# Ranks and allowances in a planned instruction order: softmax maximum and exponential first, later dates for what follows them

## Chip, cores, metric

One core of one Trainium2 chip. The time is device microseconds of one execution; lower is better. The kernel before took 956.38 us (median of three runs, 956.17 to 956.78).

## What is computed

Block-causal attention, then two MLPs, in fp32:

```python
scores = scale * q @ k.T            # 4 batches, 8 heads, 576 rows, head size 64
scores = where(block_i >= block_j, scores, -1e9)      # blocks of 64
attn = exp(scores - max) / (sum + 1e-9)
x = (attn @ v) as (2304, 512)
x = leaky(x @ w_in) @ w_out         # 512 -> 2048 -> 512, leak 0.01
out = silu(x @ w2_in) @ w2_out
```

## The kernel before

**Stages.** The 2304 tokens are cut into six blocks of 384 (0 to 5). The first MLP of a block is 16 steps: a first layer (L1427 to L1429), its gate on ACT (L1475), a high and a low part of the gated value (g_hi on ACT or DVE, g_lo on DVE, L384), and a second layer (L1447). Every fp32 product of block 1 and later is three matmuls of high and low parts. While the layers of block b run, the attention of block b+1 is worked in between them; a block's first layer needs that block's whole x. Block 0 and the attention of block 1 use a simpler form (`start`, `pair_unit`); blocks 2 to 5 use `unit`. After the attention (some 520 us into the span) come the rest of the first MLP and the second MLP (L1681 to L1683, L1844), which the change does not touch.

**One unit of attention** (`unit`, L1053) is up to 128 query rows of one head, or the last 64 rows of two heads. Its chain, with the names used below:
- **scores**, PE, L1084, into one of two PSUM banks `s`; 576 keys are done as two pieces of 288
- **max**, DVE: memset of the masked corner (L1092), then the reduction (L1094; L1096 and L1098 for two pieces)
- **exp**, ACT, L1102, out of the bank, which is then free for the scores after next
- **norm**, DVE, L1109 to L1112
- **p_hi**, ACT or DVE, L1116 or L1118, then **p_lo**, DVE, L1121
- a transposing DMA by the queue of SP, L1130
- **weighing** (`weigh_all`, L1198), PE, L1145 to L1147, all units of a group into the one bank `x`
- **x_top**, ACT or DVE, L858 or L860, then **x_sum**, DVE, L864: the two halves of that bank, evacuated and added; the next group's weighing waits for them
- x in a high and a low part (L373 or L375, then L384 `l<-x,h`), which the first layer reads

A head's keys and queries are loaded by SP (L792, L830) and split in parts by ACT and DVE (k_lo is L384 `k<-kqr,k`, q_lo L807).

**The order** is made on the host by `Schedule` (L69). Every piece of work is a task with engines and modelled durations, the tasks it needs, and a rank. The planner steps through modelled time. When a task ends, its users may be ready after a hop (`HOP`) plus the task's `lag`; a task joins its engine's queue when it has been ready for `slack` ns; a free engine takes the lowest rank that waits:

```python
heapq.heappush(waiting, (t.ready + t.slack + (self.HOLD if n else 0), order[id(t)], n, e, t))
...
u.ready = max(u.ready, t.end + (self.HOP[e] + t.lag if u in t.users else 0))
```

What comes out is a fixed order of instructions on each engine; the waits in the program are those of the data. So ranks, lags and slacks change no wait and no duration, they only change places in the order. Gates and their parts have rank GATE (-1000) plus their step, scores, weighings, transposes and x_top/x_sum SHORT (-500) plus a rank, the rest of the attention its plain rank (60 and more). Before the change scores and weighings have a slack of 700, max and exp the plain rank, and lags exist only on loads and transposes.

Of the kernel before, what the change touches and what calls it, by code (L numbers as in the profile page):

```python
# [38 lines left out]
SLACK = 700  # L39
# [10 lines left out]
ORDER = (1, 2, 6, 7, 5, 4, 3)  # L50
BEHIND, LAG = 6, 2500
KQ_LAG, V_LAG, PT_LAG = 2500, 2500, 1500
KQR, KR, QR, VR = 960, 1728, 2048, 1792
PR, HLR, PTR = 1408, 2304, 2304

# [140 lines left out]
def freed(*regions):  # L196

    return [t for r in regions for o in r.before for t in o.users]
# [35 lines left out]
def attn_mlp_mlp(  # L234
# [103 lines left out]
    plan = Schedule()  # L338


    def act(n, psum=False, pointers=0):
        return 0.833 * n + (52 if psum else 94) + 93 * pointers

    def dve(n, pointers=0):
        return Both(1.042 * n + 68 + 61 * pointers)

    def dve_psum(n):
        return 1.042 * n + 68

    def dve2x(n, pointers=0):  # L350
        return Both(0.521 * n + 68 + 61 * pointers)

    def mm(n):
        return max(107, n / 2.4) + 13.5
# [22 lines left out]
    def copy_on(n, psum=False):  # L377
        return {"ACT": act(n, psum), "DVE": dve_psum(n) if psum else dve2x(n)}
# [346 lines left out]
    def attention(blk):  # L725
# [6 lines left out]
        def rank_at(k):  # L732
            first = blk == 1
            return (blk - 1 + k / n_ticks * (ATT1 if first else ATT_SLOPE)) * NF + (ATT0 if first else ATT)
# [113 lines left out]
        def take(hd, both, group, at, t0, t1, done_by):  # L848

            d0 = D * (hd.h % 2)  # L850
            cols, to = slice(at, at + t1 - t0), slice(t0 - hd.q0, t1 - hd.q0)

            def x_top(e):
                if both.x is None:
                    both.x = rp.tile([P, NB], F32, tag="x32", name="x32")
                o, i = both.x[d0 : d0 + D, to], group.x[D:, cols]
                if e == "ACT":
                    nc.scalar.activation(o, i, AF.Copy, scale=1.0 / PS)  # L858
                else:
                    nc.vector.tensor_scalar(o, i, 1.0 / PS, None, op0=ALU.mult)  # L860

            def x_sum(e):
                o = both.x[d0 : d0 + D, to]
                nc.vector.scalar_tensor_tensor(  # L864
                    o, group.x[:D, cols], 1.0 / PS, o, op0=ALU.mult, op1=ALU.add
                )

            rk = SHORT + rank_at(done)
            t_top = plan.add(copy_on(t1 - t0, True), [*done_by, *(pairs[-1] if pairs else ())], rk, x_top)
            t_sum = plan.add({"DVE": dve_psum(t1 - t0)}, [t_top], rk, x_sum)  # L870
            group.evac.append(t_sum)
            both.evac.append(t_sum)
# [18 lines left out]
        def two_heads(hds, both):  # L891

            nonlocal done
            assert hds[0].q0 == 0 and hds[0].q1 % P == 0
            chunks = hds[0].q1 // P
            for cs in (range(chunks - 1), range(chunks - 1, chunks)):
                before = groups[-1] if groups else None
                groups.append(Group())
                group, width = groups[-1], len(cs) * P
                for n, c in enumerate(cs):  # L900
                    pair_unit(hds, c * P, (n * P, width + n * P), rank_at(done), group)
                    done += 2 * P
                done_by = weigh_all(group, before)
                for j in (0, 1):
                    take(hds[j], both, group, j * width, cs[0] * P, cs[-1] * P + P, done_by)
            take_pair(hds[0], both)

        for i in range(0, len(todo), 2):
# [21 lines left out]
            for bank in banks:  # L930
                before = groups[-1] if groups else None
                groups.append(Group())
                group, at, cols = groups[-1], 0, []
# [119 lines left out]
    def unit(parts, per, rk, group, group_before):  # L1053

        u = Unit()
# [4 lines left out]
        w = n // n_pieces  # L1060
# [5 lines left out]
        r_st = st_ring.take(8)  # L1066
# [11 lines left out]
        def scores(e, piece):  # L1078
            k0, k1 = cut[piece]
            s = u.s[piece] = next_s()  # L1080
            for i, (hd, c0, _) in enumerate(parts):
                c = c0 - hd.q0
                for j, a in enumerate((c, hd.np + c)):
                    nc.tensor.matmul(  # L1084
                        s[:, :w], hd.q[:, a : a + P], hd.k[:, k0:k1],
                        start=i + j == 0, stop=i == len(parts) - 1 and j == 1,
                    )

        def row_max(e, piece):
            last = piece == n_pieces - 1  # L1090
            if per > BLK and last:
                nc.vector.memset(u.s[-1][:BLK, w - BLK : w], MASKED)  # L1092
            if n_pieces == 1:
                nc.vector.tensor_reduce(nm[:rows], u.s[0][:rows, :n], axis=AX.X, op=ALU.max, negate=True)  # L1094
            else:
                nc.vector.reduce_max(m2[:rows, piece : piece + 1], u.s[piece][:rows, :w], axis=AX.X)  # L1096
                if last:
                    nc.vector.tensor_reduce(nm[:rows], m2[:rows], axis=AX.X, op=ALU.max, negate=True)  # L1098

        def expo(e, piece):  # L1100
            k0, k1 = cut[piece]
            nc.scalar.activation(  # L1102
                p[:rows, k0:k1], u.s[piece][:rows, :w], AF.Exp, bias=nm[:rows], accum_out=s2[:rows, piece : piece + 1]
            )
# [46 lines left out]
        t_max, s_last = [], before.t_s if before else None  # L1151
        for i in range(n_pieces):
            def first(e, i=i):
                scores(e, i)

            def second(e, i=i):
                row_max(e, i)

            deps = [*split, *s_users[-2]] if len(s_users) > 1 else [*split]
            time = 2 * m * mm(w)  # L1160
            u.t_s = s_last = plan.add({"PE": time}, deps, SHORT + rk, first, [s_last] if s_last else ())
            s_last.slack = SLACK
            s_users.append([])
            masked = 165 if per > BLK and i == n_pieces - 1 else 50
            time = masked + dve_psum(w) + (150 if n_pieces > 1 and i else 0)
            t_max.append(plan.add({"DVE": time}, [u.t_s, *t_max, *(() if i else freed(r_st))], rk, second))
        u.t_max = t_max[-1]
        deps = [u.t_max, *freed(r_p)]
        for i in range(n_pieces):
            def third(e, i=i):  # L1170
                expo(e, i)

            u.t_exp = plan.add({"ACT": act(w, True, 2)}, deps, rk, third, [u.t_exp] if i else ())
            s_users[i - n_pieces].append(u.t_exp)
            deps = []
        u.t_norm = plan.add({"DVE": 290 + 90 * (n_pieces - 1)}, [u.t_exp], rk, norm)
        u.t_hi = plan.add(
            {"ACT": act(n, False, 1), "DVE": dve2x(n, 1)}, [u.t_norm, *freed(r_hl)], rk, p_hi, first_units
        )
        u.t_lo = plan.add({"DVE": dve(n, 1)}, [u.t_hi], rk, p_lo)  # L1180
        padded_keys = [u.t_lo]
        if n % P:
# [15 lines left out]
    def weigh_all(group, before):  # L1198

        us = group.units  # L1200
        deps = [t for u in us for t in (u.t_turn, *[t for hd in u.heads for t in hd.v_ready])]
        deps += before.evac if before else [x0_free]

        def values(e):
            for u in us:
                u.values(e)

        t = plan.add({"PE": sum(u.pv_time for u in us) + TRANSIT}, deps, SHORT + us[-1].rk, values)
        t.slack = 0 if group.units[0].native else SLACK
        for u in us:  # L1210
            u.t_pv = t
            u.r_pt.users.append(t)
            for hd in u.heads:
                hd.rv.users.append(t)
        return [t]
# [819 lines left out]
```

## Time and profile before

| | us |
|---|---|
| median of three runs | 956.38 |
| the profiled execution | 956.43 |
| its span, first to last instruction | 954.7 |
| PE busy | 932.2 |
| DVE busy | 808.5 |
| ACT busy | 557.8 |

The profile's busy share of PE counts modelled matmul durations, which overlap; a stop shorter than that overlap isn't seen in it. PEld is the loading of weights, which runs ahead of PE. A line of the timeline or of a group ends, in brackets or behind a bar, with the idle time of the engine just before it and what ended it. In the table of waits the columns are: engine and instruction that waited, what released it, total us, number of times, longest us.

### The profile page before, as it was taken

What the parts mean: (1) busy time and instruction counts of PE and PEld (TensorE: products, weight loads), DVE (VectorE), ACT (ScalarE), POOL (GpSimd) and SP (SyncE); (2) the same over time, 40 slices, a digit from 0 to 9 for tenths busy, and PEclk for the clock granted to TensorE, in tenths of its full rate; (3) what the DMA queues carried; (4) which work ended last, traced back from release to release, by engine and by line L of the source; (5) the groups of instructions that cost most, each with busy time, mean ns of one, the idle gap of its engine ahead of it and who ended that gap; (6) DMA issues with size and microseconds to landing.
All of it is one profiled execution on the core that took longest, in us unless ns stands there. A gap on an engine that the chain in (4) does not pass through costs nothing.

```text
span 954.7 us, 18424 instructions
## 1 busy us (share of the span) xinstructions
PE 932.2 (98%) x6565; PEld 857.5 (90%) x6565; DVE 808.5 (85%) x1885; ACT 557.8 (58%) x1256; POOL 36.0 (4%) x127
## 2 busy tenths in 40 slices
PE   9999999999999999999999999999999999999997
PEld 4556669898899998999999999999999999999997
DVE  6999899988777788888775897989899999888965
ACT  6987758666665676767465765656455642222222
POOL 1000000100000000000000000000000000000000
PEclk9999999999999999999999999999999999999999
DMA  7777728576545575675444633579846544443412
GB/s 228 221 191 209 206 66 186 108 143 122 151 106 110 126 159 140 121 139 152 97 110 112 206 122 125 198 244 311 287 172 232 185 139 138 129 154 111 144 56 89
DMA packets 193771, 149.05 MB, mean 156 GB/s; under 512 B 134160, under 2 KB 171792, under 8 KB 193680
## 3 DMA queue, kind: packets, MB, share of 16 engines
q1 hardware_dynamic: 193680, 147.89, 56.4%
q8 instruction: 51, 0.84, 0.4%
q14 instruction: 40, 0.33, 0.1%
HBM read 90.70 MB, written 32.51 MB: 129 GB/s over the span
## 4 chain that ended last, share of the span: by engine, by line
PE 47%; DVE 8%; ACT 3%; issue 2%; DMA 0%; DVEq 0%; ACTq 0%
PE acc L1844 7%; PE s L1844 5%; PE acc L1447 4%; PE acc L1681 3%; PE acc L1682 3%; PE acc L1683 3%; PE x L1844 2%; PE u L1844 2%; PE s L1681 2%; PE s L1682 2%; PE h L1427 2%; PE s L1683 2%; PE h L1429 2%; PE h L1428 2%; PE u L1447 1%
## 5 line engine op out<-in xcount | busy, mean ns | idle before, releaser
L1102 ACT ACTIVATE p<-s,st 128x288 f32<-128x288 f32 (+4 forms) x120 | 62.2, 520 | 53.5 <-DVE st L1094 28.7
L1116 ACT ACTIVATE hl<-p,st 128x576 f16<-128x576 f32 (+5 forms) x91 | 55.9, 617 | 38.5 <-DVE st L1112 19.5
L1121 DVE SCALAR_TENSOR_TENSOR hl<-p,st,hl 128x576 f16<-128x576 f32 (+4 forms) x96 | 60.1, 627 | 18.6 <-ACT hl L1116 14.5
L1084 PE MATMUL s<-k,q 128*128 128x288 f32 (+5 forms) x288 | 66.7, 326 | 9.1 <-ACT p L1102 5.4
L1447 PE MATMUL acc<-ghi,w 128*128 128x384 f32 x255 | 67.1, 339 | 0.0
L1084 PEld LDWEIGHTS s<-k,q 128*128 128x128 f32 x288 | 46.4, 189 | 19.4 <-ACT p L1102 14.0
L1475 ACT ACTIVATE g<-h 128x384 f32<-128x384 f32 x96 | 46.5, 484 | 26.2 <-PE h L1429 24.2
L1427 PE MATMUL h<-h,w 128*128 128x384 f32 x180 | 60.9, 338 | 0.0
L1733 ACT ACTIVATE e<-e 128x384 f32<-128x384 f32 (+1 forms) x72 | 42.7, 626 | 26.2 <-DVE e L1706 20.8
L384 DVE TENSOR_TENSOR glo<-g,ghi 128x384 fp32r<-128x384 f32 x80 | 44.2, 553 | 12.3 <-ACT ghi L373 11.8
L1145 PE MATMUL x<-raw,v 128*128 128x128 f16 (+1 forms) x384 | 54.4, 209 | 0.2
L420 ACT ACTIVATE cy<-raw 128x512 f32<-128x512 f32 x64 | 43.1, 674 | 18.5 <-DVE w L442 6.5
L1429 PE MATMUL h<-h,w 128*128 128x384 f32 x160 | 53.7, 335 | 0.0
L1146 PE MATMUL x<-raw,v 128*128 128x128 f16 (+1 forms) x384 | 53.6, 208 | 0.0
L1428 PE MATMUL h<-l,w 128*128 128x384 f32 x160 | 53.6, 335 | 0.0
L1147 PE MATMUL x<-raw,v 128*128 128x128 f16 (+1 forms) x384 | 53.2, 209 | 0.0
L864 DVE SCALAR_TENSOR_TENSOR x<-x,x 64x128 f32<-64x128 f32 (+3 forms) x96 | 30.3, 315 | 19.6 <-ACT x L858 18.2
L1447 PEld LDWEIGHTS acc<-ghi,w 128*128 128x128 f32 x255 | 44.8, 188 | 0.3
L384 DVE TENSOR_TENSOR v<-v 128x320 f32<-128x320 f32 (+5 forms) x112 | 44.2, 424 | 0.3
L1145 PEld LDWEIGHTS <-v 128*128 128x128 bf16 x384 | 36.7, 98 | 5.4 <-issue 4.9
L1447 PE MATMUL acc<-glo,w 128*128 128x384 f32 x120 | 40.3, 336 | 0.0
L373 ACT ACTIVATE ghi<-g 128x384 fp32r<-128x384 f32 x76 | 39.6, 521 | 1.1
(385 smaller groups left out, 3080.9 us busy)
## 6 DMA issues: line engine op xcount, KB each, us to landing
raw<-w SPq DMA_DIRECT2D x64, 512.0 KB, 4.6
raw<-g SPq DMA_DIRECT2D x64, 256.0 KB, 3.1
g<-e SPq DMA_DIRECT2D x48, 192.0 KB, 3.1
g<-e SPq DMA_DIRECT2D x24, 384.0 KB, 3.4
kqr<-kq_l SPq DMA_DIRECT2D x16, 480.0 KB, 3.5
kqr<-kq_l SPq DMA_DIRECT2D x16, 416.0 KB, 3.3
v<-vL SPq DMA_DIRECT2D x32, 160.0 KB, 3.2
y<-yT SPq DMA_DIRECT2D x12, 384.0 KB, 3.7
```

The lines of the kernel that those rows point to most:

```text
L384: engine[e].tensor_tensor(lo, x, hi, op=ALU.subtract)
L1084: nc.tensor.matmul(s[:, :w], hd.q[:, a : a + P], hd.k[:, k0:k1], start=i + j == 0, stop=i == len(parts) - 1 and j == 1,)
L1102: nc.scalar.activation(p[:rows, k0:k1], u.s[piece][:rows, :w], AF.Exp, bias=nm[:rows], accum_out=s2[:rows, piece : piece + 1])
L1116: nc.scalar.activation(hl[:rows, 0, :n], p[:rows], AF.Copy, scale=rc[:rows])
L1121: nc.vector.scalar_tensor_tensor(hl[:rows, 1, :n], p[:rows], rc[:rows], hl[:rows, 0, :n], op0=ALU.mult, op1=ALU.subtract)
L1145: nc.tensor.matmul(g.x[:, o], a, hi, start=j == 0, stop=False)
L1146: nc.tensor.matmul(g.x[:, o], hd.vb[:, j], hi, start=False, stop=False)
L1427: nc.tensor.matmul(h, w1_lo[s.f][:, sl], hi[:, c, : s.n], start=c == 0, stop=False)
L1428: nc.tensor.matmul(h, w1_hi[s.f][:, sl], lo[:, c, : s.n], start=False, stop=False)
L1429: nc.tensor.matmul(h, w1_hi[s.f][:, sl], hi[:, c, : s.n], start=False, stop=c == NC - 1)
L1447: nc.tensor.matmul(s.acc[c][:, : s.n], a, b, start=s.f == 0 and i == 0, stop=s.f == NF - 1 and i == 2)
L1844: nc.tensor.matmul(o, a[:, x], b, start=i == 0 and j == 0 and q == 0, stop=i == NP - 1 and q == 2, skip_group_check=True,)
```

## The change

Six constants and what uses them. Max and exp of a `unit` get the rank CHAIN + rk, that is 100 lower, so that a free engine takes them ahead of other attention work. The slack of scores goes from 700 to 300. Four kinds of task get a lag, by which the planner takes what follows them to be ready later: weighing 800, x_top 400 (not in block 1), norm 300, p_hi 300. (The lag of `t_hi` is on p_hi; its user is p_lo.)

```diff
+CHAIN = -100.0
+S_SLACK = 300
+PV_LAG, TOP_LAG, NORM_LAG, HI_LAG = 800, 400, 300, 300
...
             t_top = plan.add(copy_on(t1 - t0, True), [*done_by, *(pairs[-1] if pairs else ())], rk, x_top)
+            t_top.lag = 0 if blk == 1 else TOP_LAG
...
-            s_last.slack = SLACK
+            s_last.slack = S_SLACK
...
-            t_max.append(plan.add({"DVE": time}, [u.t_s, *t_max, *(() if i else freed(r_st))], rk, second))
+            t_max.append(plan.add({"DVE": time}, [u.t_s, *t_max, *(() if i else freed(r_st))], CHAIN + rk, second))
...
-            u.t_exp = plan.add({"ACT": act(w, True, 2)}, deps, rk, third, [u.t_exp] if i else ())
+            u.t_exp = plan.add({"ACT": act(w, True, 2)}, deps, CHAIN + rk, third, [u.t_exp] if i else ())
...
+        u.t_norm.lag, u.t_hi.lag = NORM_LAG, HI_LAG
...
-        t.slack = 0 if group.units[0].native else SLACK
+        t.slack, t.lag = (0, 0) if group.units[0].native else (SLACK, PV_LAG)
```

## Rows read from the trace of the kernel before

**Rows 1.** The page, part 1: busy time, share, instructions.

```profile
span 954.7 us, 18424 instructions
...
PE 932.2 (98%) x6565; PEld 857.5 (90%) x6565; DVE 808.5 (85%) x1885; ACT 557.8 (58%) x1256; POOL 36.0 (4%) x127
```

**Rows 2.** Windows: stretch, length, busy us by engine, granted clock, DMA share, GB/s.

```profile
120.00:520.00 400.00, 389.34 (x3040) 365.35 (x3039) 330.21 (x954) 262.21 (x685) 30.04 (x110) 1.00 0.57 125
```

**Rows 3.** Waits of PE's matmuls, 120 to 520 us.

```profile
PE s L1084 <- ACT p L1102: 5.4, 10, 1.4
PE s L1084 <- DVE k L384: 3.1, 5, 1.1
...
PE h L1428 <- DVE l L384: 0.5, 1, 0.5
```

**Rows 4.** Line 1084, scores: idle before them (us, times), PEld and PE together.

```profile
ACT p L1102: 19.4, 33
DVE k L384: 3.6, 7
ACT h L373: 2.8, 2
```

**Rows 5.** Timeline of PE around one stop: start us, length us.

```profile
169.47 0.33 PE L1447 MATMUL u<-ghi,e 128*128 128x384 f32 x1
169.64 0.34 PE L1447 MATMUL u<-glo,e 128*128 128x384 f32 x1
171.37 0.53 PE L1084 MATMUL s<-k,q 128*128 128x288 f32 x2 [1.39 <-ACT p L1102]
171.74 0.34 PE L1427 MATMUL h<-h,w 128*128 128x384 f32 x1
```

**Rows 6.** Waits of ACT, 120 to 520 us.

```profile
ACT p L1102 <- DVE st L1094: 28.7, 34, 3.2
ACT p L1102 <- DVE st L1098: 24.3, 22, 3.2
ACT hl L1116 <- DVE st L1112: 19.5, 24, 2.1
ACT x L858 <- PE x L1147: 13.4, 8, 3.6
```

**Rows 7.** Waits of DVE, 120 to 520 us.

```profile
DVE x L864 <- ACT x L858: 16.9, 21, 3.1
DVE hl L1121 <- ACT hl L1116: 14.5, 25, 1.0
...
DVE s L1092 <- PE s L1084: 2.0, 1, 2.0
```

**Rows 8.** Timeline of DVE, 212 to 214 us.

```profile
212.35 0.82 DVE L1121 SCALAR_TENSOR_TENSOR hl<-p,st,hl 128x576 f16<-128x576 f32 x1 [0.72 <-ACT hl L1116]
213.08 0.55 DVE L384 TENSOR_TENSOR glo<-g,ghi 128x384 fp32r<-128x384 f32 x1
...
213.78 0.49 DVE L1094 TENSOR_REDUCE st<-s 128x1 f32<-128x320 f32 x1
```

**Rows 9.** Timelines of PE and ACT beside it.

```profile
211.30 0.54 PE L1084 MATMUL s<-k,q 128*128 128x320 f32 x2
...
214.98 0.54 PE L1084 MATMUL s<-k,q 128*128 128x288 f32 x2 [0.62 <-ACT p L1102]
...
214.31 0.53 ACT L1102 ACTIVATE p<-s,st 128x320 f32<-128x320 f32 x1 [1.48 <-DVE st L1094]
```

**Rows 10.** The page, part 5: the exponentials of the units.

```profile
L1102 ACT ACTIVATE p<-s,st 128x288 f32<-128x288 f32 (+4 forms) x120 | 62.2, 520 | 53.5 <-DVE st L1094 28.7
```

**Rows 11.** Waits of SP's queue, 120 to 520 us: transposes.

```profile
SPq L1130 <- DVE hl L1121: 88.4, 54, 4.1
```

**Rows 12.** Lines 1084 and 1145: durations (ns), first and last start us.

```profile
L1084 PE MATMUL s<-k,q x288: 221/296/657, 127.1 to 505.3; 128*128 128x288 f32 x64, 128*128 128x320 f32 x16, 128*128 128x448 f32 x16, 128*128 128x512 f32 x16
L1145 PE MATMUL x<-raw,v x384: 192/219/233, 155.5 to 515.9; 128*128 128x128 f16 x104, 128*128 128x64 f16 x88
```

**Rows 13.** Timeline of DVE and PE where block 3's first layer begins.

```profile
331.44 0.36 DVE L384 TENSOR_TENSOR l<-x,h 128x192 fp32r<-128x192 f32 x1
...
331.85 0.44 PE L1428 MATMUL h<-l,y 128*128 128x384 f32 x1 [0.46 <-DVE l L384]
```

## The prediction

> **What bounds the kernel now.** I read the page's busy shares first, then the busy time by stretches, then the waits of each engine inside the stretch that the change can reach, and last a timeline of single stops. PE is busy for 932.2 of 954.7 us [rows 1], so it sets the time, and only PE's stops can be won. The change touches blocks 2 to 5 of the attention alone, which run from about 120 to 520 us; there PE is busy for 389.34 of 400 us at a granted clock of 1.00, the 2.4 GHz level [rows 2]. Idle is 400 - 389.34 = 10.7 us. The reader should see how small this is: a perfect order in this stretch gains one or two per cent, no more.
>
> What are the stops? Of PE's matmul waits the largest is scores waiting for an exp, the next scores waiting for k_lo [rows 3]. Both rows together hold 8.5 of the 10.7 us. PE with its weight loads taken together shows more of them: before scores, 19.4 us in 33 stops for an exp, 3.6 us in 7 for k_lo, 2.8 us in 2 for an x part: 25.8 us in 42 stops [rows 4]. The two totals differ because matmul durations overlap. In one stop [rows 5] the layer's matmuls start 0.17 us apart (169.47, 169.64) and are each shown as 0.33 to 0.34 us long, so each stop hides about 0.17 us, and here 1.39 us of idle cost 171.37 - 169.64 - 0.17 = 1.56 us. With 42 stops I put the loss at 10.7 + 42 x 0.17 = 17.8 us, between 10.7 and 25.8. The exp's share by its part in the loads' idle is 19.4 / 25.8 = 0.75: **13.4 us**, with the ends 0.75 x 10.7 = 8.0 and 19.4. After the stop, the layer's matmuls that stood behind the scores start at once (171.74): they were ready.
>
> Here the Trainium skill ("Perfetto Trace Analysis", section Identifying the Most-Contended Engine) says that matmul busy time is a poor measure of distance to the bound and the busy share of weight loads a better one. By that rule the room in this stretch would be 400 - 365.35 = 34.6 us [rows 2] and the exp's share 26 us, my estimate from that page's rule. I keep 13.4, because the loads' idle also holds time in which matmuls were still queued.
>
> **Why the exps are late.** ACT stood idle before them, waiting for the max, for 28.7 us in 34 cases and 24.3 us in 22 [rows 6]: 56 of 120 exps [rows 10]. So DVE had the max late, though it is not full: 330.2 busy of 400 [rows 2]. DVE itself stands still inside its fixed order: 16.9 us for x_top in 21 cases and 14.5 us for p_hi in 25 [rows 7]. One case shows how these join [rows 8, 9]. Scores of 320 columns are done at 211.84 (211.30 + 0.54). DVE waits 0.72 us for p_hi, does p_lo, then g_lo, and starts the max only at 213.78, 1.94 us after the scores. The exp follows 0.04 us after the max, and PE, which wanted the bank, stands 0.62 us until 214.98.
>
> **The change, part by part.**
> - **Max and exp 100 lower in rank.** No instruction is added. In the case above the max passes p_lo and its wait: 213.08 - (212.35 - 0.72) = 1.45 us earlier; it does not pass g_lo, whose rank is lower still. p_lo then comes later by a memset and a reduction, some 0.65 us (213.63, where g_lo ends, to 214.27). Its transpose waits behind it on SP, which already stands 88.4 us for p_lo in 54 cases [rows 11], and loads of keys and values are queued behind the transposes. I cost this at nothing: the weighings begin 28 us after the scores and end 10.6 us after them [rows 12], so there is more than 10 us of work between. If that lead is used up, each of 96 transposes would pass up to 0.65 us on to a weighing, 62 us; nothing near it fits 10 us of lead.
> - **Four lags.** They take a follower off the place where it stops its engine. Mean waits today [rows 6, 7]: x_sum 16.9 / 21 = 0.80 against a lag of 0.4; p_lo 14.5 / 25 = 0.58 against 0.3; p_hi 19.5 / 24 = 0.81 against 0.3; x_top 13.4 / 8 = 1.68 against 0.8. Each covers 0.37 to 0.52 of its mean wait. So about half of 64.3 us of standing in ACT's and DVE's orders goes, between none (other work put there waits too) and all. None of it is PE time by itself; it comes through earlier exps.
> - **Slack 700 to 300.** Scores are placed up to 0.4 us earlier, so a bank must be free 0.4 us earlier too. On a stop that stays this adds up to 0.4 us.
> - The lags make the planned chain 0.8 + 0.4 + 0.3 + 0.3 = 1.8 us longer per unit. Inside a block the lead of 10 us covers it; at a block's end see the second rival.
>
> **The sum.** Where the max was queued behind other DVE work, it comes 1.45 us earlier and the scores 0.4 us: net 1.05 us, against a mean stop of 19.4 / 33 = 0.59 us. Such a stop goes. ACT's rows say that 56 of 120 exps, 47%, were of this kind; I take half of the stops. On the other half, 0.4 us less slack stands against lags of 0.3 to 0.8 us, and I count neither. So half of 13.4 us goes: 6.7 us, between nothing (or the loss of the third rival) and 13.4. From the profiled execution, 956.43 us (1.7 more than its span, and 0.05 from the median), that is **949.7 us**.
>
> **Rivals.**
> 1. *All of it.* Max, exp and lags clear every stop for an exp: 956.4 - 13.4 = 943.0. For: 53 us of ACT's idle before exps has one cause. Against: g_lo and the gates still pass the max, and two banks are as few as before.
> 2. *Given back at the block ends.* A block's first layer needs the last pair's x. It stood 0.46 us for a low part that ended at 331.80 [rows 13], so there the attention has no lead. If the longer chain shows in full, four blocks cost 4 x 1.8 = 7.2 us, and the gain of 6.7 turns into +0.5: 956.9, no change. Against: this is the only such stop in the list [rows 3], 0.5 us, and lags delay only what another task overtakes.
> 3. *Scores too early, slower.* PE's order puts the scores in front of layer matmuls that are ready [rows 5]. If the max comes no earlier in effect, because what it passes was not what held it, each of the 33 stops gets 0.4 us longer: 13.2 us by the loads' count, and by 17.8 / 25.8 about 9.1 us on PE: 965.5. It decides once max plus exp gain less than 0.4 us on average. For: the max itself can then stop DVE waiting for scores; against: that happened once so far, 2.0 us [rows 7], and the one case read closely gains 1.45. The Trainium skill ("PSUM — Partial Sum Buffer", section Engine vs sequencer instructions) states that matmuls start in program order. By that rule the layer's matmuls cannot step past waiting scores, which is this rival's mechanism. The trace agrees: 1.39 us of idle with L1427 right behind.
>
> **Chances.** About 0.2% (1.9 us) is what a measurement can tell from no change. Forecast, between 945 and 954.4: 0.54. First rival, below 945: 0.12. Second, 954.5 to 958.3: 0.16. Third, above 958.3: 0.18. So faster 0.66, same 0.16, slower 0.18. The range, 942 to 959, holds the forecast, more than half of the first rival, the second, and the near end of the third, some 0.8 of the chance.
>
> **What would show it.** Right: idle before scores for an exp falls from 19.4 us in 33 stops to about half; ACT's 53 us before exps falls by at least as much; DVE's waits for x_top and p_hi, 31 us together, fall by half; PE's busy time from 120 to the attention's end comes closer to the stretch, which ends some 6 us sooner; what follows keeps its length. Wrong: exps earlier but PE's stops moved to x parts at block ends (second rival), or more stops before scores with mean above 0.6 us (third).

## The result, and the profile after

The changed kernel takes 947.16 us (median of five runs, 946.88 to 949.66) against 956.38 us before; the ratio is 0.9909, with a 95% interval of 0.9894 to 0.9923. The gain is 9.2 us, where 6.7 was forecast.

The page of the changed kernel, part 1, answers to [rows 1]:

```profile
span 945.8 us, 18395 instructions
...
PE 927.6 (98%) x6565; PEld 857.6 (91%) x6565; DVE 808.8 (86%) x1897; ACT 552.6 (58%) x1244; POOL 37.1 (4%) x127
```

The work is the same but for 12 instructions that passed from ACT to DVE: DVE is busy for 808.8 us as before, PE's weight loads for 857.6. The span is 8.9 us shorter. The same stretch as in [rows 2], by the view of windows:

```profile
120.00:520.00 400.00, 394.39 (x3093) 374.82 (x3093) 336.50 (x978) 262.56 (x684) 31.21 (x110) 1.00 0.58 131
```

PE's idle in it falls from 10.7 to 5.6 us, that of its weight loads from 34.6 to 25.2, and 53 more matmuls fit into the 400 us. Where the gain ends is best read from the first matmul of the second MLP (line 1681 before, 1686 after; columns: durations in ns, first and last start in us). Before:

```profile
L1681 PE MATMUL x<-x,w x48: 333/334/335, 585.8 to 758.2; 128*128 128x384 f32 x48
```

After:

```profile
L1686 PE MATMUL x<-x,w x48: 334/334/343, 576.7 to 749.1; 128*128 128x384 f32 x48
```

The start comes 9.1 us sooner, and from there to the end both need the same time (954.7 - 585.8 = 368.9 and 945.8 - 576.7 = 369.1). So the whole gain lies ahead of the second MLP, as forecast.

What stood before the scores, PE and its weight loads together, answers to [rows 4]:

```profile
ACT p L1106: 13.1, 22
DVE k L387: 1.7, 3
ACT g L1480: 0.7, 1
```

The 25.8 us in 42 stops are 15.5 us in 26. The stops for an exp lost a third (19.4 to 13.1), those for k_lo half, and the two for an x part are gone. The only waits of PE's matmuls themselves, against [rows 3]:

```profile
PE s L1088 <- ACT p L1106: 4.6, 7, 1.2
PE s L1088 <- DVE k L387: 0.9, 2, 0.5
```

In this stretch no layer matmul waits any more, at a block's end or elsewhere. DVE's waits, against [rows 7]; x_top is L861 on ACT and L863 on DVE, x_sum L867:

```profile
DVE glo L387 <- ACT ghi L376: 15.3, 12, 3.6
DVE hl L1125 <- ACT hl L1120: 7.2, 11, 1.1
DVE x L863 <- ACT x L861: 5.6, 6, 2.1
DVE x L867 <- ACT x L861: 5.5, 5, 2.7
```

x_sum's wait falls from 16.9 to 5.5 us (with the x_tops on DVE it is 11.1), p_lo's from 14.5 to 7.2; in exchange g_lo waits longer for its high part, which before was:

```profile
DVE glo L384 <- ACT ghi L373: 6.2, 8, 1.9
```

ACT before the exps, against [rows 6] and the 53.5 us of [rows 10]:

```profile
ACT p L1106 <- DVE st L1098: 28.2, 41, 1.8
...
ACT p L1106 <- DVE hl L1125: 14.5, 11, 2.1
...
ACT p L1106 <- DVE st L1102: 9.1, 8, 2.5
ACT hl L1120 <- DVE st L1116: 8.9, 12, 3.4
ACT x L861 <- PE x L1151: 8.2, 8, 2.2
```

ACT's idle before exps has not fallen: 28.2 + 14.5 + 9.1 = 51.8 us here, 53.0 before. Of it 37.3 us in 49 cases are waits for the max, so these did fall. The 14.5 us in 11 cases are new: there an exp stands until an earlier unit's p_lo (L1125) has read the buffer `p` that it writes to. That ACT's idle falls was to be the sign that the rank works. So three questions were open: which of the three parts carries the gain, whether they need each other, and how much is the luck of another order.

### The profile page after: what moved, and what is told of

Its sections match the earlier page's. It is cut to its first block, busy times and chain, and to the rows that moved or that the text cites. A ratio compares the mean times of both kernels' runs of the same rounds, so it can differ in the third digit from the quotient of the medians.

```text
span 945.8 us, 18395 instructions
## 1 busy us (share of the span) xinstructions
PE 927.6 (98%) x6565; PEld 857.6 (91%) x6565; DVE 808.8 (86%) x1897; ACT 552.6 (58%) x1244; POOL 37.1 (4%) x127
## 4 chain that ended last, share of the span: by engine, by line
PE 49%; DVE 2%; issue 0%; ACT 0%; DVEq 0%
PE acc L1849 8%; PE s L1849 5%; PE acc L1452 5%; PE acc L1686 3%; PE acc L1688 3%; PE acc L1687 3%; PE x L1849 2%; PE u L1849 2%; PE h L1432 2%; PE h L1434 2%; PE h L1433 2%; PE s L1686 2%; PE s L1688 2%; PE s L1687 2%; PE u L1452 2%; PE x L1688 1%
## 5 line engine op out<-in xcount | busy, mean ns | idle before, releaser
L1106 ACT ACTIVATE p<-s,st 128x288 f32<-128x288 f32 (+4 forms) x120 | 62.5, 522 | 53.9 <-DVE st L1098 28.2
L1120 ACT ACTIVATE hl<-p,st 128x576 f16<-128x576 f32 (+5 forms) x87 | 52.8, 616 | 24.6 <-DVE st L1116 8.9
L1125 DVE SCALAR_TENSOR_TENSOR hl<-p,st,hl 128x576 f16<-128x576 f32 (+4 forms) x96 | 59.1, 623 | 7.9 <-ACT hl L1120 7.2
L387 DVE TENSOR_TENSOR glo<-g,ghi 128x384 fp32r<-128x384 f32 x80 | 44.2, 552 | 18.3 <-ACT ghi L376 17.5
L387 DVE TENSOR_TENSOR v<-v 128x320 f32<-128x320 f32 (+4 forms) x112 | 44.9, 423 | 0.7
L1098 DVE TENSOR_REDUCE st<-s 128x1 f32<-128x320 f32 (+3 forms) x72 | 36.3, 504 | 2.3
```

What stands on the lines that cost most here:

```text
L387: engine[e].tensor_tensor(lo, x, hi, op=ALU.subtract)
L1106: nc.scalar.activation(p[:rows, k0:k1], u.s[piece][:rows, :w], AF.Exp, bias=nm[:rows], accum_out=s2[:rows, piece : piece + 1])
L1125: nc.vector.scalar_tensor_tensor(hl[:rows, 1, :n], p[:rows], rc[:rows], hl[:rows, 0, :n], op0=ALU.mult, op1=ALU.subtract)
```

## Experiments

All kernels are the changed one with other constants, so that its lines hold. Times are medians; "against before" is the difference to the kernel before in the same set of runs (medians 956.37 to 956.97).

**Rank alone.**

```diff
-S_SLACK = 300
-PV_LAG, TOP_LAG, NORM_LAG, HI_LAG = 800, 400, 300, 300
+S_SLACK = 700
+PV_LAG, TOP_LAG, NORM_LAG, HI_LAG = 0, 0, 0, 0
```

> Ranks alone (CHAIN -100; scores' slack 700 and no lags, as before). My theory: max passes p_lo and what it waits for, so the idle of PE and its weight loads before scores for an exp falls from 19.4 us to about 12, and without the earlier scores nothing is given back: 951 to 953 us. Rival, lags do it: within 2 us of before, 954.5 to 958. Rival, luck of a new order: anything from 946 to 960, with stops of other kinds in the place of those removed.

Measured: 958.31 us, 1.0019 (1.0010 to 1.0028), slower, though by less than an order without meaning moves (below). Idle before scores for an exp is 21.0 us in 35 stops. DVE's waits in this kernel:

```profile
DVE x L867 <- ACT x L861: 21.1, 22, 3.8
DVE hl L1125 <- ACT hl L1120: 14.3, 24, 1.0
```

With the max first and nothing else, DVE stands as long as before at p_lo and longer at x_sum. My theory of the rank falls.

**Earlier scores alone.**

```diff
-CHAIN = -100.0
-PV_LAG, TOP_LAG, NORM_LAG, HI_LAG = 800, 400, 300, 300
+CHAIN = 0.0
+PV_LAG, TOP_LAG, NORM_LAG, HI_LAG = 0, 0, 0, 0
```

> Scores' slack 300 alone (plain ranks, no lags). My theory: scores come up to 0.4 us earlier with no earlier exp, so 33 stops grow: slower by 3 to 9 us, 959 to 965, idle before scores for an exp above 22 us. Rival, earlier scores give the attention a lead that it lacked: faster by 2 to 5 us, 951 to 954, with more stops before scores but none at layer matmuls.

Measured: 956.48 us, 0.9999 (0.9991 to 1.0008). Neither: 19.8 us in 36 stops for an exp against 19.4 in 33. The feared loss of 9 us is not there, nor a gain.

**Lags alone** (CHAIN 0, S_SLACK 700).

> The four lags alone (plain ranks, slack 700). My theory: DVE's waits for x_top and p_hi, 31 us together before, fall by half, exps come earlier in part: 952 to 955. Rival, the longer chain shows at the block ends: 955 to 960, with PE waiting for x parts where a block's first layer begins. Rival, the lags are the whole gain: 947 to 949.

Measured: 954.67 us, 0.9982 (0.9973 to 0.9990). As forecast in size, but the second MLP's first matmul starts at 581.1 us, 4.7 sooner than before: 372.1 us are left from there to the end, where the changed kernel has 369.1, so part of the gain was lost behind it. DVE's waits:

```profile
DVE x L867 <- ACT x L861: 6.2, 6, 2.7
DVE hl L1125 <- ACT hl L1120: 6.1, 12, 1.0
...
DVE x L863 <- ACT x L861: 2.5, 6, 0.7
```

Against 31 us before these are 14.8: a half, as the prediction worked out. But in 325 to 340 us this kernel ran with a lower clock (window of that stretch):

```profile
325.00:340.00 15.00, 11.82 (x69) 11.01 (x70) 12.16 (x41) 9.58 (x26) 1.79 (x7) 0.77 0.69 150
```

A granted clock of 0.77 over 15 us costs at most 15 x 0.23 = 3.4 us of full-speed time; PE stood for some of it.

**Without the earlier scores** (S_SLACK 700, the rest as changed).

> Ranks and lags without the earlier scores (slack 700). My theory: the earlier scores cost up to 0.4 us on each stop that is left (22 in the changed kernel), so without them it is as fast or faster: 944 to 947.5. Rival, the earlier scores are a needed part: 950 to 953, the attention of blocks 3 to 5 ending later against the layers.

Measured: 947.96 us, 0.9909 (0.9895 to 0.9923), the changed kernel's own ratio; 9.6 us in 18 stops for an exp. In these two settings the slack is worth nothing that can be measured.

So far rank alone gave +1.6, lags alone -2.0 and both -8.7 us. A second theory, that they need each other, was set against the luck of the order.

**Without the rank** (CHAIN 0, the rest as changed).

> The changed kernel without the rank (CHAIN 0): lags and slack 300. New theory, rank and lags need each other (rank alone gained nothing, lags alone 1.8 us, both 8.7): 952 to 956, as with the lags alone. Rival, luck of the order: no relation to the runs before, anything from 945 to 960.

Measured: 949.40 us, 0.9927 (0.9910 to 0.9943): faster than the theory allowed, 7.0 us against before.

**Without the lags** (all four 0, the rest as changed).

> The changed kernel without the lags: rank and slack 300. New theory, rank and lags need each other: 955 to 959, as with the rank alone, and DVE's waits for x_top and p_hi stay at 30 us or more together. Rival, luck of the order: anything from 945 to 960.

Measured: 957.03 us, 1.0002 (0.9993 to 1.0011), as expected; the waits for x_top and p_hi are 30.1 us.

**Two orders that mean nothing**: S_SLACK 310 in the changed kernel, and 660 in the setting of before (CHAIN 0, no lags). Each moves some two hundred instructions or more on every compute engine.

> The changed kernel with the scores' slack 310 in place of 300: a change of no meaning that still gives another order in all engines' lists. New theory: 945.5 to 949.5. Rival, luck of the order: 950 or more, as likely as not.

> The kernel before with the scores' slack 660 in place of 700: again only another order. New theory: 954.5 to 958.5. Rival, luck of the order: below 952 or above 960 is as likely as not.

Measured: 950.02 us, 0.9936 (0.9922 to 0.9951), and 953.29 us, 0.9971 (0.9961 to 0.9980). Both lie outside what the second theory gave, the first where its rival has it, the second between the two. A new order with no purpose moves the time by 3 us, up or down: 947.16 to 950.02 and 956.38 to 953.29. With two such orders the scatter is known only roughly, but differences of this size between single kernels say nothing about a part. Adding the lags gave 7 to 10 us in three of four pairs (957.03 to 947.16, 958.31 to 947.96, 956.48 to 949.40), above that scatter, and 1.7 in the fourth (956.38 to 954.67).

A third theory follows: the lags carry the gain, rank and slack little. It was tested by the lags alone in another order, by each pair of lags, and by twice their size.

**Lags alone, another order** (CHAIN 0, S_SLACK 660).

> The lags alone once more (plain ranks), in another order by the scores' slack 660. Third theory, the lags carry the gain and rank and slack change little beyond the 3 us by which a new order moves the time: the attention and the first MLP end (first L1686) at 574 to 580 us, total 946 to 951. Rival, rank and lags need each other: 953 to 957, first L1686 at 581 or later.

Measured: 951.21 us, 0.9942 (0.9927 to 0.9956), first L1686 at 576.9 us. By that start the third theory holds, the time just misses its upper end. Against before it is 3.8 us better than the other kernel with the lags alone, so the order matters here as much as without lags. With the nudge of before (953.29) it makes a fifth pair for the lags: in the profiled executions the second MLP starts 7.6 us sooner (584.5 to 576.9), but the total is only 2.7 us better against before (-3.1 to -5.8). Part of the difference was lost behind that start, where the clock was lower for some us (see behind the table).

**Lags on weighing and x_top only; on norm and p_hi only.**

```diff
-PV_LAG, TOP_LAG, NORM_LAG, HI_LAG = 800, 400, 300, 300
+PV_LAG, TOP_LAG, NORM_LAG, HI_LAG = 800, 400, 0, 0
...
+PV_LAG, TOP_LAG, NORM_LAG, HI_LAG = 0, 0, 300, 300
```

> The changed kernel with the lags on weighing and x_top only (norm and p_hi 0). Third theory, each pair of lags takes its own stops away: DVE's wait for x_top stays near 11 us or less, that for p_hi goes back to about 14; first L1686 at 578 to 583, total 948 to 954. Rival, the x lags are the whole gain (single waits up to 3.1 us were there): 576 to 578, total 946 to 949.

> The changed kernel with the lags on norm and p_hi only (weighing and x_top 0). Third theory: DVE's wait for x_top goes back to 17 to 21 us, that for p_hi stays near 7; first L1686 at 579 to 584, total 950 to 955. Rival, the p lags are the whole gain: 576 to 578, total 946 to 949.

Measured: 950.98 us, 0.9936 (0.9921 to 0.9951), first L1686 at 580.4; and 954.95 us, 0.9983 (0.9973 to 0.9993), at 584.5. DVE's waits with the x lags:

```profile
DVE hl L1125 <- ACT hl L1120: 8.8, 18, 1.0
DVE x L867 <- ACT x L861: 8.7, 6, 3.7
```

and with the p lags:

```profile
DVE x L867 <- ACT x L861: 20.0, 22, 3.7
...
DVE hl L1125 <- ACT hl L1120: 3.5, 7, 0.7
```

The wait for p_hi did not go back to 14 with the x lags, but it is not at 14 in the kernel to compare with either: rank and slack without lags have 20.5 us at x_sum and 8.5 at p_lo. Against that one each pair removes its own stops. The x lags give 6.0 us against before, the p lags 2.0, no more than luck, and their second MLP starts just later than forecast. The single stops at x_sum are longer, up to 3.7 us here, where a p_hi costs DVE 1.0 us at most.

**Lags doubled** (1600, 800, 600, 600).

> All four lags doubled (1600, 800, 600, 600), the rest as in the changed kernel. Third theory: each lag covered about half of its mean wait, so the rest goes too: DVE's waits for x_top and p_hi together fall from 18 to below 8 us, first L1686 at 572 to 577, total 942 to 947. Rival, the longer planned chain takes it back at the block ends: PE waits for x parts, total 948 to 954.

Measured: 957.07 us, 0.9999 (0.9988 to 1.0009). DVE's waits for x_top and p_hi fall to 13.9 us, less far than forecast, and the gain is gone; the total lies above the rival's range too. The timeline of PE near block 3's start shows where:

```profile
326.02 0.22 PE L1149 MATMUL x<-raw,v 128*128 128x128 f16 x1 [2.29 <-issue]
...
327.35 1.65 PE L1088 MATMUL s<-k,q 128*128 128x320 f32 x4 [0.48 <-DVE k L387]
329.68 0.85 PE L1088 MATMUL s<-k,q 128*128 128x288 f32 x2 [0.68 <-ACT p L1106]
331.56 0.85 PE L1088 MATMUL s<-k,q 128*128 128x288 f32 x2 [1.03 <-ACT p L1106]
332.21 0.52 PE L1432 MATMUL h<-h,y 128*128 128x384 f32 x1
332.53 0.52 PE L1433 MATMUL h<-l,y 128*128 128x384 f32 x1
```

Between block 2's layers, which end at 323.7, and block 3's, which begin at 332.21, PE's order holds only the block's last weighing and scores. The weighing comes after 2.3 us of standing, for which the profile shows no releaser, and from 327.35 on PE is slow: two matmuls of 288 columns take 0.85 us, where they took 0.53 in [rows 5], and the layer's start 0.32 us apart instead of 0.17. The windows:

```profile
310.00:325.00 15.00, 13.73 (x121) 13.21 (x119) 9.81 (x28) 8.34 (x22) 0.41 (x2) 1.00 0.54 116
325.00:340.00 15.00, 11.78 (x78) 10.57 (x79) 13.99 (x45) 8.96 (x24) 1.97 (x6) 0.66 0.37 90
340.00:355.00 15.00, 15.00 (x124) 14.84 (x122) 12.41 (x39) 9.46 (x25) 1.47 (x7) 1.00 0.91 204
```

A clock of 0.66 costs at most 15 x 0.34 = 5.1 us, less for the time that PE stood. The changed kernel in the same 15 us:

```profile
325.00:340.00 15.00, 14.54 (x111) 14.03 (x110) 14.36 (x45) 11.27 (x33) 1.66 (x6) 1.00 0.59 160
```

111 matmuls against 78. First L1686 is 584.2 - 576.7 = 7.5 us later than in the changed kernel; this one place holds most of it: block 3's first layer begins at 332.21 us, in the changed kernel at 328.46, and the rest of the slow stretch comes on top.

All runs together (waits in us, 120 to 520 us; "DVE at x, p" is what DVE waits for x_top and p_hi, "rest" the span behind the first L1686):

| kernel | rank | slack | lags x, p | against before | first L1686 | exp stops | DVE at x, p | rest |
|---|---|---|---|---|---|---|---|---|
| before | 0 | 700 | none | 0 | 585.8 | 19.4 | 31.7 | 368.9 |
| e1 | -100 | 700 | none | +1.6 | 587.5 | 21.0 | 36.6 | 369.1 |
| e2 | 0 | 300 | none | -0.2 | 585.4 | 19.8 | 29.1 | 369.1 |
| e6 | -100 | 300 | none | +0.7 | 585.6 | 17.7 | 30.1 | 370.4 |
| e8 | 0 | 660 | none | -3.1 | 584.5 | 21.1 | 31.0 | 368.7 |
| e3 | 0 | 700 | x, p | -2.0 | 581.1 | 15.6 | 14.8 | 372.1 |
| e9 | 0 | 660 | x, p | -5.8 | 576.9 | 13.7 | 16.5 | 372.1 |
| e5 | 0 | 300 | x, p | -7.0 | 574.8 | 12.2 | 16.5 | 373.7 |
| e4 | -100 | 700 | x, p | -8.7 | 573.9 | 9.6 | 12.3 | 370.5 |
| after | -100 | 300 | x, p | -9.2 | 576.7 | 13.1 | 18.3 | 369.1 |
| e7 | -100 | 310 | x, p | -6.4 | 577.1 | 11.6 | 18.1 | 370.2 |
| e10 | -100 | 300 | x | -6.0 | 580.4 | 15.1 | 17.5 | 369.2 |
| e11 | -100 | 300 | p | -2.0 | 584.5 | 17.8 | 24.6 | 368.7 |
| e12 | -100 | 300 | doubled | +0.1 | 584.2 | 14.7 | 13.9 | 370.2 |

The five kernels without lags average -0.2 us, the six with all four at their size -6.5. In total they touch (-3.1 in e8, -2.0 in e3). By the start of the second MLP, in the profiled executions, they do not: 584.5 to 587.5 and 573.9 to 581.1.

The rest is not the same in all of them: the change does not touch the second MLP, but its order can still come out another way, and the clock can fall in it. In the three kernels with lags and without the rank it is 372.1 to 373.7 us. In all three the granted clock fell there, and in e3 and e9 at the start of block 3 as well. Windows of e9, then of e5, then of e3:

```profile
325.00:330.00 5.00, 3.09 (x13) 3.01 (x14) 4.64 (x17) 2.21 (x7) 0.86 (x2) 0.81 0.89 179
330.00:335.00 5.00, 5.00 (x27) 5.00 (x26) 4.14 (x12) 2.94 (x9) 0.20 (x1) 0.84 0.34 66
770.00:775.00 5.00, 3.50 (x18) 3.47 (x18) 4.73 (x8) 2.10 (x3) 0.00 (x0) 0.69 0.79 241
...
580.00:585.00 5.00, 3.46 (x14) 2.97 (x14) 1.63 (x4) 3.37 (x7) 0.00 (x0) 0.85 1.04 398
585.00:590.00 5.00, 5.00 (x25) 5.00 (x25) 3.21 (x7) 1.63 (x4) 0.00 (x0) 0.81 0.47 142
770.00:775.00 5.00, 4.01 (x21) 4.02 (x22) 4.73 (x8) 2.10 (x3) 0.00 (x0) 0.66 0.79 242
...
775.00:780.00 5.00, 4.33 (x23) 4.33 (x24) 4.73 (x9) 2.10 (x3) 0.00 (x0) 0.66 0.72 216
```

Length times what the clock lacks adds up to at most 3.5 us in e9, 3.4 in e5 and 5.1 in e3. The three kernels with lags and rank (e4, after, e7) have no such stretch in their profiled executions. Without lags e6 has one (590 to 600 us, at most 1.7 us).

## Why the prediction was right, and where not

- **Where the time is.** Right: PE's stops before scores in 120 to 520 us were the only thing to win, the work and the later stages kept their length. 949.7 was forecast, 947.16 came; the first rival, every exp stop gone, did not come, since 13.1 us of them are left.
- **The size.** Two terms were off and nearly cancel, so that the number came near was in part luck. The sum let half of the exp's stops go and priced them at 17.8 / 25.8 = 0.69 of the idle that PE and its weight loads show. The runs give the full idle: the loads add up to 857.5 us before and 857.6 after, so what the span loses, their idle loses. In the stretch that is 9.5 us (34.6 to 25.2), against 9.1 at the start of the second MLP; e4 has 12.0 against 11.9, e5 11.3 against 11.0. The matmuls' idle falls by 5.1 only, as their modelled durations add up to less (932.2 and 927.6). By this measure the exp's stops were worth 19.4 us and not 13.4. A third of them went and not half, 6.3 us. The rest came from stops that I had left as they were: k_lo 3.6 to 1.7 us, x parts 2.8 to 0, the layer's own waits 1.3 to 0.
- **The lags.** Right, and more than I gave them: half of DVE's and ACT's stops at x_sum, p_lo, p_hi and x_top was forecast to go; 64.3 us became 35.4 (5.5 + 5.6 + 7.2 from DVE's rows, the x_tops on DVE included, 8.9 + 8.2 from ACT's). What I called a help to the rank is the carrier: without lags there is no gain in four kernels but the 3.1 us of a chance order. But the standing was moved more than removed. Against the 28.9 us that these four lose, g_lo's wait for g_hi grows by 9.1 us, max's for scores by 4.8 and exp's for p_lo by 14.5; in the stretch ACT is busy for 262.6 us as before (262.2), DVE for 336.5 against 330.2.
- **The rank.** This step failed. "The max passes p_lo and its wait, 1.45 us earlier" was read from one case and taken for the half of all. Alone the rank gives no gain (+1.6 us, inside the scatter of orders), and with it x_sum's wait grows from 16.9 to 21.1 us (20.5 in e6); that what the max passes stands later, in the same order, is my reading. ACT's 53 us before exps, which were to fall, stayed in sum. The delay of p_lo, costed at nothing because its transpose has a lead, shows in another place: exps stand 14.5 us for p_lo in the changed kernel. It is 0.2 us in the rank alone, so the lags have a part in it. With the lags in place the rank's kernels average -8.1 us against -4.9 without it (three each), but the three without it lost at most 3.4 to 5.1 us each to the clock, and the starts of their second MLP mix (574.8 to 581.1 without, 573.9 to 577.1 with). Whether the rank adds something there stays open.
- **The slack.** I costed it at nothing net; three pairs say so (against before: 0 and -0.2, +1.6 and +0.7, -8.7 and -9.2). In the fourth, lags without rank, slack 300 is 5.0 us better (-2.0 and -7.0); both kernels lost time to the clock, and this stays open. The third rival, with the slack as a loss of up to 9.1 us, is refuted: e2 is its own test. The wait that it feared on DVE, max standing for scores, does grow, from 2.0 us in one case to 4.3 + 2.5 us in 12 ([rows 7] and the list of who waits for scores below), without harm to the time. It is larger still with slack 700 (11.9 us in e4), so it isn't the slack that makes it.
- **The block ends.** The second rival is not there at the lags' size, no layer matmul waits for x. At twice the size, in the one order measured, the gain is lost at such a place, as that rival said, though through a late weighing, late scores and the clock; PE's matmuls wait 0.2 us for an x part.

Line 1088 in the changed kernel, who waited for it:

```profile
DVE s L1096: 4.3, 7
DVE st L1100: 2.5, 5
```

Why fewer stops on DVE mean fewer on PE, while ACT still stands 52 us before exps, is argued and not shown: the planner's order for PE fits if ACT and DVE keep the modelled pace, and a lag as long as half the real wait moves the model toward it. That PE's stops of all three kinds shrink with the lags, and not with the rank, speaks for this; that the places to which the standing moved hold PE less is argued too.

## What to carry to other kernels

Where a planner fixes the order, read on the secondary engines which instruction stands waiting for another engine, and let the model end the task it waits for later; that was worth more here than ranks. A lag of half the measured mean wait was a good size here; twice that, in the one order tried, lost the whole gain. Price PE's stops by the idle of its weight loads, whose sum stayed the same, and not by that of modelled matmuls. Before crediting a part, measure a change without meaning (here such a one moved the time by 3 us) and compare the granted clock.

## What was unexpected of the hardware

The granted clock fell to 1.2 GHz, the lower of its two levels, where PE's order ran thin, and stayed there after layer matmuls were under way again. In the doubled lags PE stood 2.29 us, did a weighing, stood 0.48 us, and was slow from there: 0.66 on average over 325 to 340 us. In the lags alone 0.77 followed stops of 0.45, 1.02 and 1.81 us within 5 us at the same block start; in their other order (e9) 0.81 and 0.84 followed one stop of 3.36 us there, and the first layer matmuls behind it still started 0.17 us apart. The single stop of 1.39 us of [rows 5], between layer matmuls, left the stretch at 1.00.

That the stops are the cause is argued from these places, and they do not decide it alone. In the second MLP six kernels with lags have the same two stops, of 0.37 and 1.50 us. Behind them the clock fell in e3, e5 and e9 and not in e4, e7 and e12. The second stop and the window behind it, in e3 and in e4:

```profile
775.67 0.38 PE L1849 MATMUL acc<-w,l 128*128 128x256 f32 x1 [1.50 <-DVE l L387]
775.00:780.00 5.00, 4.33 (x23) 4.33 (x24) 4.73 (x9) 2.10 (x3) 0.00 (x0) 0.66 0.72 216
...
768.50 0.38 PE L1849 MATMUL acc<-w,l 128*128 128x256 f32 x1 [1.50 <-DVE l L387]
770.00:775.00 5.00, 5.00 (x44) 5.00 (x43) 4.73 (x9) 1.94 (x3) 0.00 (x0) 1.00 0.43 132
```

What else decides is open. One such place costs at most 1.6 to 5.1 us, as much as half of the change's gain, and explains part of the scatter between orders.
